# Sliding-window attention and a mixture of adapters on one core: Q kept by rows, a longer warm-up, the last group in halves, and a new written-out order

## The chip, the cores and the metric

The kernel runs on one core of a Trainium2 chip. A core has five engines that run side by side and wait for each other by semaphores: TensorE (PE: matmuls and the weight loads ahead of them), VectorE (DVE), ScalarE (ACT), GpSimd (POOL) and SyncE (SP). Each works through its own instructions strictly in order. Transfers between memory (HBM) and the on-chip SBUF are issued from an engine's queue and run on 16 DMA engines that all queues share. Matmuls write to PSUM, which the kernel uses as 8 banks of 512 float32 words a partition.

The metric is the time of one execution in microseconds (us), as the device reports it.

## What is computed

Inputs are q, k and v of shape (8, 8, 576, 64): batch, heads, sequence, width, in float32. Attention is limited to a window of 32 positions to each side. Its output, with heads side by side as x of 4608 rows and 512 columns, goes through a mixture of 8 adapters of rank 16, of which each row takes the two with the largest logits:

```
scores = q @ k.T / sqrt(64);  scores[|i - j| > 32] = -1e9
x      = (softmax(scores) @ v), heads side by side        # [4608, 512]
logits = x @ w_gate;  top 2 of 8;  w = softmax of these two
out    = x + sum over the two e of  w[e] * ((x @ A[e]) @ B[e])
```

## The kernel before, in words

A unit is one batch entry and head. The 64 units are laid out as two halves of partitions (g = 0, 1: batch entries 0 to 3 and 4 to 7) of 32 units, and these are worked off in two passes p = 0, 1 of NU = 16 units. The 576 rows are cut into NB = 9 blocks of 64.

Loading (`load_qk`, `load_v`). Q and K come in tiles t of 128 rows for 16 units of each half, t = 0 to 3 for pass 0, t = 4 to 7 for pass 1, and t = 8 (`XT`) holds what is left at the ends of all units. One tile is two loads of 256 KB (four of 128 KB for Q's t = 8), issued from POOL's queue (L305), which turn float32 into float16 on the way. V's tiles come as four loads of 128 KB each (L383). For t in `DIRECT` = (0, 1, 8), PE transposes the raw tile itself (L319, 16 transposes of 64 columns for each half hf); for the others POOL, now and then ACT, first brings it into another order (`cast`, L331 and L329), and PE takes 8 transposes of 128 columns for a half (L339). ACT or DVE then copies PSUM into qT or kT in SBUF (`evict`, L356). POOL or ACT copies the end rows of Q from xq into qT (`ends`, L365). DVE transposes V (L391). qT lies as [partition, unit, row], so one unit's rows are adjacent; a pair of rows lies as one float32 word, and evictions move words.

Scores (`score`). For each pass, block a and half of the units, PE adds the window's mask (two matmuls of 512 columns with the constants mask and twice, L425) and then, for 8 units and both g, multiplies K's block with the 64 to 128 Q rows that can see it (L435: 16 matmuls, 32 for the block in the middle, where Q goes from one qT tile to the next). ACT takes the exponential into PT (L444). There are 36 such score groups.

PV (`pv`). For each pass and group g of 128 rows (five groups of a pass), PE multiplies PT with V and a column of ones, in three portions of 6, 5 and 5 units (L480); DVE takes the reciprocal of the sums (L491) and multiplies into x (L497).

Adapters (`moe`), once for each of the 10 groups, over four tiles of 128 rows: PE transposes x (L526), ACT copies (L181), PE multiplies with the adapters' A and w_gate (L566), DVE takes maximum and differences (L576, L577), ACT the exponential (L584), DVE seven small operations (L590 to L597) and the product with the gates (L607), PE transposes (L616), ACT or DVE copies (L181, L179), PE multiplies with B (L640), and x is added. That last step goes two ways for each pair of row tiles: where `BY_PE` (L684) says so, PE adds x through a matmul with the identity (L643) and ACT or DVE only copies to ob (L651); elsewhere DVE adds (L654). SP stores ob (L661), 40 stores in all.

The order of all this is written out. The functions above only record operations in a `Plan`; `ORDER` is the list in which `Plan.give` emits all 566 of them, `ON` picks the engine of each that can go to two, and `HOME` gives each buffer its place in its pool (raw tiles, cast tiles c16, PSUM banks B, x, and so on; pool sizes in `POOLS`). No operation may be emitted before those that make what it needs, or before the last holder of its buffer is done. The waits themselves are set by the recording layer below, from which part of a tile an instruction touches: where the ranges of addresses of two accesses overlap, the later one waits, even if the two leave out each other's elements. Loads from POOL use 8 semaphores in turn, and a load waits until the one before it on its semaphore has landed.

At the start PE runs `WARM` = 4 matmuls of 512 columns in float32 on zeros (L222).

## Time and profile before

| | us |
|---|---|
| median of 3 runs | 130.28 |
| lowest and highest | 129.54, 130.38 |
| the profiled execution | 131.63 |
| its span, first to last instruction | 129.7 |

The profile records that one execution. Its page has the busy time of each engine; the span in 40 slices of 3.24 us, each digit the busy share in tenths; the DMA queues; the chain of work that ended last, followed back from the end, as shares; and groups of instructions by line. PEld are PE's weight loads. A row of the timeline reads: start, duration, engine, line, what is written and read, the count of instructions, and in brackets the idle time before it with what ended it. A row of the windows reads: stretch, its length, the busy time of each engine with its instructions, the clock that TensorE was granted (1 is full speed), the DMA engines' share, and what they moved. A row of the groups ends in busy time, mean ns of one, and idle time before it by what ended it.

### The profile page before, as it was taken

What the parts mean: (1) busy time and instruction counts of PE and PEld (TensorE: products, weight loads), DVE (VectorE), ACT (ScalarE), POOL (GpSimd) and SP (SyncE); (2) the same over time, 40 slices, a digit from 0 to 9 for tenths busy, and PEclk for the clock granted to TensorE, in tenths of its full rate; (3) what the DMA queues carried; (4) which work ended last, traced back from release to release, by engine and by line L of the source; (5) the groups of instructions that cost most, each with busy time, mean ns of one, the idle gap of its engine ahead of it and who ended that gap; (6) DMA issues with size and microseconds to landing.
All of it is one profiled execution on the core that took longest, in us unless ns stands there. A gap on an engine that the chain in (4) does not pass through costs nothing.

```text
span 129.7 us, 5424 instructions
## 1 busy us (share of the span) xinstructions
PE 110.1 (85%) x2354; PEld 80.8 (62%) x2354; DVE 90.9 (70%) x204; ACT 81.2 (63%) x127; POOL 65.0 (50%) x119
## 2 busy tenths in 40 slices
PE   6904987978899999979699999999999999988620
PEld 3204955657778667667595577899767677855200
DVE  4000605749995899959779579979799896898830
ACT  6001354959868758965577978678868976644430
POOL 6879619629896999194983386991000000000000
PEclk9997579999999999999999999999999999999996
DMA  4999996999999999999999999989025036365684
GB/s 91 195 199 211 209 187 95 164 192 203 184 194 214 192 135 234 212 231 281 251 254 206 215 251 203 157 233 323 27 61 181 13 121 224 111 199 189 234 287 181
DMA packets 13542, 24.47 MB, mean 189 GB/s; under 512 B 3024, under 2 KB 3024, under 8 KB 13520
## 3 DMA queue, kind: packets, MB, share of 16 engines
q0 software_dynamic: 6944, 14.16, 61.5%
q1 hardware_dynamic: 5248, 9.44, 20.7%
q10 hardware_dynamic: 1328, 0.54, 1.8%
q8 instruction: 18, 0.29, 0.9%
q14 instruction: 4, 0.03, 0.1%
HBM read 28.85 MB, written 9.44 MB: 295 GB/s over the span
## 4 chain that ended last, share of the span: by engine, by line
PE 49%; DMA 26%; POOL 11%; ACT 4%; issue 4%; DVE 1%; SPq 0%; POOLq 0%
DMA raw<-in_q_dram 24%; PE banks L435 9%; PE banks L480 8%; PE banks L566 6%; PE banks L339 6%; PE banks L526 5%; PE banks L640 5%; POOL raw L305 5%; PE banks L425 4%; POOL c L331 3%; PE banks L319 3%; POOL v L383 3%; ACT ob L651 2%; PE banks L643 2%; DMA out_dram<-ob 2%
## 5 line engine op out<-in xcount | busy, mean ns | idle before, releaser
L444 ACT ACTIVATE PT<-banks 128x1024 f16<-128x1024 f32 x36 | 35.8, 1025 | 9.9 <-PE banks L435 9.0
L331 POOL COPY c<-raw 128x1024 f16<-128x1024 f16 x22 | 22.9, 1066 | 8.9 <-DMA raw<-in_k_dram 3.8
L497 DVE TENSOR_TENSOR x<-banks,rc 128x640 f16<-128x640 f32 (+1 forms) x30 | 25.8, 866 | 0.9
L435 PE MATMUL banks<-qT,kT 64*64 64x128 f16 (+2 forms) x640 | 23.0, 214 | 1.4 <-DVE qT L356 0.8
L435 PEld LDWEIGHTS <-kT 64*64 64x64 f16 x640 | 17.4, 108 | 10.4 <-issue 9.2
L383 POOL DMA_DIRECT2D v<-in_v_dram x36 | 18.4, 522 | 5.7 <-DMA raw<-in_k_dram 3.9
L480 PE MATMUL banks<-vt,PT 64*128 64x65 f16 x832 | 17.4, 190 | 1.7 <-issue 0.9
L391 DVE STREAM_TRANSPOSE vt<-v 128x1024 f32<-128x1024 f32 x9 | 18.7, 2080 | 0.1
L480 PEld LDWEIGHTS <-PT 64*128 64x128 f16 x832 | 14.3, 94 | 4.9 <-issue 3.0
L339 PE MATMUL banks<-ident,c 128*128 128x128 f16 x192 | 13.9, 220 | 2.2 <-issue 1.1
L425 PE MATMUL banks<-mask,twice 64*128 64x512 f16 x72 | 14.4, 389 | 0.4 <-issue 0.3
L640 PE MATMUL banks<-Bw,zT 128*128 128x512 f16 x40 | 13.0, 382 | 1.4 <-ACT zT L181 1.4
L654 DVE TENSOR_TENSOR ob<-banks,x 128x1024 f32<-128x1024 f32 x11 | 13.4, 1217 | 0.6 <-PE banks L640 0.4
L339 PEld LDWEIGHTS <-c 128*128 128x128 f16 x192 | 11.2, 98 | 3.8 <-issue 1.3
L356 DVE COPY qT<-banks 128x512 f32<-128x512 f32 x3 | 2.0, 670 | 16.2 <-PE banks L319 16.2
L319 PE MATMUL banks<-ident,raw 128*64 128x128 f16 x192 | 8.4, 251 | 4.8 <-DMA raw<-in_q_dram 4.8
L305 POOL DMA_DIRECT2D raw<-in_q_dram x20 | 10.8, 560 | 2.6 <-DMA raw<-in_q_dram 1.2
L491 DVE RECIPROCAL rc<-banks 128x10 f32<-128x10 f32 (+1 forms) x30 | 6.4, 215 | 8.1 <-PE banks L480 6.1
L356 ACT COPY kT<-banks 128x512 f32<-128x512 f32 x16 | 9.3, 594 | 4.3 <-PE banks L339 3.4
L526 PE MATMUL banks<-ident,x 128*128 128x128 f16 x160 | 11.5, 220 | 0.2 <-DVE x L497 0.2
L181 ACT COPY xT<-banks 128x512 f32<-128x512 f32 x20 | 11.2, 593 | 0.6 <-PE banks L526 0.4
L356 ACT COPY qT<-banks 128x512 f32<-128x512 f32 x13 | 7.5, 594 | 6.4 <-PE banks L339 3.8
(55 smaller groups left out, 135.3 us busy)
## 6 DMA issues: line engine op xcount, KB each, us to landing
out_dram<-ob SPq DMA_DIRECT2D x24, 256.0 KB, 4.3
raw<-in_k_dram POOLq DMA_DIRECT2D x18, 256.0 KB, 7.2
v<-in_v_dram POOLq DMA_DIRECT2D x36, 128.0 KB, 6.4
raw<-in_q_dram POOLq DMA_DIRECT2D x16, 256.0 KB, 7.8
out_dram<-ob SPq DMA_DIRECT2D x16, 192.0 KB, 3.9
raw<-in_q_dram POOLq DMA_DIRECT2D x4, 128.0 KB, 5.5
ob<-in_moe_A_dram ACTq DMA_DIRECT2D x1, 256.0 KB, 3.0
ob<-in_moe_B_dram ACTq DMA_DIRECT2D x1, 256.0 KB, 5.6
```

The costliest lines, as they stand in the source:

```text
L331: (nc.vector if eng == "DVE" else nc.gpsimd).tensor_copy(out=o, in_=i)
L339: nc.tensor.matmul(out=ap16(tp)[:, 128 * r:128 * r + 128], lhsT=ap(c16)[:, r], rhs=ident, is_transpose=True, start=True, stop=True)
L356: (nc.vector.tensor_copy if eng == "DVE" else nc.scalar.copy)(out=o, in_=i)
L383: op("POOL", 0.5, lambda p0=p0, src=src: nc.gpsimd.dma_start(out=ap(v16)[p0:p0 + 32], in_=src), bufs=[v16], make=[("v", t, "16")], prio=-6 ...
L391: nc.vector.transpose(out=o, in_=i)
L425: nc.tensor.matmul(out=ps_[:, 4 * j:4 * j + 4], lhsT=twice[m], rhs=bcast(mask[m], 1, 4), start=True, stop=False)
L435: nc.tensor.matmul(out=ps_[m, h, o0:o0 + c1 - c0], lhsT=ap(kT[t])[m, 64 * sl:64 * sl + 64], rhs=ap(qT[p, hq])[m, i, c0 - 288 * hq:c1 - 288 ...
L444: op("ACT", act(1024), lambda: nc.scalar.activation(out=ap(pt)[:, :, 64:192].rearrange("m i (x b r) -> m i x b r", b=2, r=16), in_=ap(ps). ...
L480: nc.tensor.matmul(out=ap(po)[:, 512 * g + VD * j:512 * g + VD * j + VD], lhsT=ap(PT[ti])[m, pos, off:off + 128], rhs=ap(vt[t])[m, sl, 0:V ...
L497: nc.vector.tensor_tensor(out=o, in0=i, in1=ap(rc)[:, 0:n].to_broadcast([128, n, 2, D]), op=ALU.mult)
L526: nc.tensor.matmul(out=ap16(tp)[:, 512 * i + 128 * c:512 * i + 128 * c + 128], lhsT=xp()[:, ab, bl].rearrange("p (m c) -> p c m", c=4)[:, ...
L640: nc.tensor.matmul(out=o, lhsT=ap(zT)[:, j + i], rhs=Bw, start=True, stop=not by_pe)
```

## The change

- `qT` is laid out as [partition, x, r, unit] instead of [partition, unit, row]: runs x of 32 rows, in these 16 pairs of rows r, in these the 16 units, and in these the pair of rows b. `evict` and `ends` write so. A score matmul reads its moving operand as pairs of float16 that lie 64 bytes apart, where it read up to 128 adjacent ones; what it writes stays.
- `WARM` goes from 4 to 8. Pool c16 goes from 6 to 7 tiles.
- The last group (pass 1, g = 4) is cut in two halves by units: four PV portions of 4 units instead of three, a second x buffer for the second half, and two calls of `moe` with two row tiles each instead of one with four.
- Which engine adds x follows from `ON`: where ACT takes the last step of a pair, PE adds x; where DVE takes it, DVE adds. In the new `ON`, ACT takes 10 of the 20 pairs and DVE 10; before, ACT took 8 and DVE 12, one of the 12 only copying.
- `ORDER`, `ON` and `HOME` are new throughout, with 576 operations. At the start the loads come as the first part of Q's tile 8, the first of K's tile 0, the rest of Q's tile 8, the second of K's tile 0, Q's tile 0, then V's tile 0, K's tile 1, Q's tile 1 (before: Q's tile 8 and tile 0 and K's tile 0 mixed, Q's tile 1, K's tile 1, V's tile 0). The copy of the first end rows goes from POOL to ACT. All four score groups of blocks 0 and 1 come ahead of the transposes of tile 1. In pass 1, Q's tiles 6 and 7 are loaded ahead of K's tiles 6 and 7, which were loaded ahead of or among them. The last operations are the two halves of group 4, where group 3 was the last.
- Of the operations with a choice, DVE takes 1 copy of Q where it took 4, 4 of K where it took 2, 2 of the transposed x where it took none and 4 of the transposed zs where it took 1. POOL casts 22 tile halves as before.

The diff without the three tables:

```diff
@@ -117,7 +119,7 @@
     assert tuple(q.shape) == (8, NH, NB * 64, D)
     DD = out.shape[1]
-    POOLS = {"B": 8, "raw": 6, "c16": 6, "v16": 3, "xq": 1,
+    POOLS = {"B": 8, "raw": 6, "c16": 7, "v16": 3, "xq": 1,
              "qT": 3, "kT": 3, "vt": 4, "PT": 8, "x": 3, "xT": 2, "zs": 2, "zT": 2, "ob": 4,
              "sm": 2, "rc": 3}
     sb = tc.alloc_tile_pool(name="sb", bufs=1)
@@ -131,7 +133,7 @@
         "c16": many("c16", [128, 8, 2 * D], F16),
         "v16": many("v16", [128, 32 * D], F16),
         "xq": many("xq", [128, 2048], F16),
-        "qT": many("qT", [128, NU, NB * 32], F16),
+        "qT": many("qT", [128, NB * 32 * NU], F16),
         "kT": many("kT", [128, 2048], F16),
         "vt": many("vt", [128, 32, VD2], F16),
         "PT": many("PT", [128, 8, 256], F16),
@@ -306,7 +308,7 @@
                 out=ap(raw)[p0:p0 + np_, g], in_=src),
                bufs=[raw], make=[(w, t, "raw")],
                prio=(-80 + due + late if t else -200 + late) + 0.01 * n,
-               dma=DMA_MB * 0.53 * np_ / 128, desc=np_)
+               dma=DMA_MB * 0.48 * np_ / 128, desc=np_)
         for hf in range(2):
             tp = buf("B", f"tp{w}{t}_{hf}")
             if t in DIRECT:
@@ -340,16 +342,15 @@
                                          rhs=ident, is_transpose=True,
                                          start=True, stop=True)
             pr = due - 22 + late + 0.1 * hf
-            op("PE", 8 * mm(128), trans, bufs=[src, tp], need=[token, "ident"],
+            op("PE", 0.58 if t in DIRECT else 8 * mm(128), trans, bufs=[src, tp], need=[token, "ident"],
                make=[(w, t, hf, "T")], prio=pr, count=n)
             def evict(eng, hf=hf, tp=tp):
                 if w == "q" and t < XT:
-                    c0 = (16, 80, 0, 64)[t % 4]
-                    o = ap(dst).bitcast(F32)[:, :, c0:c0 + 64].rearrange(
-                        "m u (x f r) -> m f u x r", f=2, r=8)[:, hf]
-                    i = ap(tp).rearrange("m (r u x) -> m u x r", r=8, u=NU)
+                    x0 = (1, 5, 0, 4)[t % 4]
+                    o = ap(dst).bitcast(F32).rearrange("m (x f r u) -> m f x r u", f=2, r=8, u=NU)[:, hf, x0:x0 + 4]
+                    i = ap(tp).rearrange("m (r u x) -> m x r u", r=8, u=NU)
                 else:
                     o = ap(dst).bitcast(F32).rearrange("m (x f r) -> m f x r", f=2, r=8)[:, hf]
                     i = ap(tp).rearrange("m (r x) -> m x r", r=8)
@@ -360,7 +361,7 @@
     def ends(p, e):
         def go(eng):
-            o = ap(qT[p, e]).bitcast(F32)[:, :, 128 * e:128 * e + 16]
+            o = ap(qT[p, e]).bitcast(F32).rearrange("m (x r u) -> m x u r", r=16, u=NU)[:, 8 * e]
             i = ap(xq).bitcast(F32).rearrange("m (e u r) -> m e u r", e=2, r=16)[:, e, NU * p:NU * p + NU]
             (nc.scalar.copy if eng == "ACT" else nc.gpsimd.tensor_copy)(out=o, in_=i)
         op({"POOL": 0.45, "ACT": act(256)}, 0, go, bufs=[xq, qT[p, e]], need=[("qT", XT)],
@@ -432,9 +433,10 @@
                     o0 = c0 - (64 * a - 32)
                     for g in range(2):
                         m = slice(64 * g, 64 * g + 64)
-                        nc.tensor.matmul(out=ps_[m, h, o0:o0 + c1 - c0],
+                        qx = ap(qT[p, hq])[m].rearrange("m (x r u b) -> m u x r b", r=16, u=NU, b=2)
+                        nc.tensor.matmul(out=ps_[m, h, o0:o0 + c1 - c0].rearrange("m (x r b) -> m x r b", r=16, b=2),
                                          lhsT=ap(kT[t])[m, 64 * sl:64 * sl + 64],
-                                         rhs=ap(qT[p, hq])[m, i, c0 - 288 * hq:c1 - 288 * hq], start=False,
+                                         rhs=qx[:, i, (c0 - 288 * hq) // 32:(c1 - 288 * hq) // 32], start=False,
                                          stop=h % 4 == 3 and c1 == hi)
         n = len(cuts) - 1
         dur = mm(512) + 0.02 + 8 * (mm(hi - lo) + 0.004 * n)
@@ -455,13 +457,14 @@
     xs = {}
     for p in range(SP):
         for g in range(5):
-            xs[p, g] = buf("x", f"x{p}{g}")
+            xs[p, g] = [buf("x", f"x{p}{g}")] * 2
+    xs[SP - 1, 4] = [xs[SP - 1, 4][0], buf("x", f"x{SP - 1}4b")]
     def pv(p, g, i0, n):
         token = (p, g, i0)
         po, rc = buf("B", f"po{token}", 2), buf("rc", f"rc{token}")
-        xd = xs[p, g]
+        xd = xs[p, g][i0 // 8]
         ops, bufs, need = [], {po}, set()
         mine = [(a, off) for a, off in ((2 * g - 1, 128), (2 * g, 64), (2 * g + 1, 0)) if 0 <= a < NB]
         for j, i in enumerate(range(i0, i0 + n)):
@@ -496,21 +499,21 @@
             o = ap(xd)[:, :, D * i0:D * (i0 + n)].rearrange("p a (n d) -> p n a d", d=D)
             nc.vector.tensor_tensor(out=o, in0=i, in1=ap(rc)[:, 0:n].to_broadcast([128, n, 2, D]), op=ALU.mult)
         op("DVE", dve32(128 * n), norm, bufs=[po, rc, xd], need=[("rc", token)],
-           make=[("x", p, g)], prio=pr)
+           make=[("x", p, g, b) for b in range(2) if i0 < 8 * b + 8 and i0 + n > 8 * b], prio=pr)
     for p in range(SP):
         for g in range(5):
-            for i0, n in ((0, 6), (6, 5), (11, 5)):
+            for i0, n in ((0, 6), (6, 5), (11, 5)) if (p, g) != (SP - 1, 4) else ((0, 4), (4, 4), (8, 4), (12, 4)):
                 pv(p, g, i0, n)
-    def moe(p, g, p0, step):
-
-        items = [(ab, bl) for bl in range(2) for ab in range(2)]
-        tok = (p, g)
+    def moe(p, g, bls, p0, step):
+
+        items = [(ab, bl) for bl in bls for ab in range(2)]
+        tok = (p, g, bls[0])
         xT = buf("xT", f"xT{tok}")
         n = len(items)
-        xd = xs[p, g]
+        xd = xs[p, g][bls[0]]
         def xp():
@@ -529,7 +532,7 @@
                             rhs=ident, is_transpose=True, start=True, stop=True)
             pr = p0 + step * 0.2 * j
             op("PE", 4 * len(two) * mm(128), turn, bufs=[xd, tp],
-               need=[("x", p, g)], make=[("tx", tok, j)], prio=pr, count=4 * len(two))
+               need=[("x", p, g, two[0][1])], make=[("tx", tok, j)], prio=pr, count=4 * len(two))
             def evict(eng, j=j, m=len(two), tp=tp):
                 o = ap(xT)[:, j:j + m].rearrange("p b c m -> p (b c m)")
@@ -539,7 +542,7 @@
                make=[("xT", tok, j)], prio=pr)
         sm = buf("sm", f"sm{tok}")
-        pzs = [buf("B", f"pz{tok}", 2)]
+        pzs = [buf("B", f"pz{tok}", n // 2)]
         zss = [buf("zs", f"zs{tok}")]
         nw = len(pzs)
@@ -576,7 +579,7 @@
                 nc.vector.tensor_reduce(out=m1[:, w], in_=lg, axis=AX.X, op=ALU.max)
                 nc.vector.tensor_tensor(out=d[:, w], in0=lg, in1=bcast(m1[:, w], 2, E),
                                         op=ALU.subtract)
-            op("DVE", 0.4, gate0, bufs=[pz, sm], need=[("pz", tok, w)], make=[("g0", tok)],
+            op("DVE", 0.36 + 0.01 * n, gate0, bufs=[pz, sm], need=[("pz", tok, w)], make=[("g0", tok)],
                prio=pr + w)
         def gexp():
@@ -595,7 +598,7 @@
             nc.vector.tensor_tensor(out=g, in0=e, in1=bcast(m2, 3, E), op=ALU.is_ge)
             nc.vector.tensor_tensor(out=e, in0=e, in1=bcast(sv, 3, E), op=ALU.mult)
             nc.vector.tensor_tensor(out=g, in0=e, in1=g, op=ALU.mult)
-        op("DVE", 1.5, gate2, bufs=[sm, pzs[0]], need=[("g2", tok)], make=[("g3", tok)], prio=pr + 1)
+        op("DVE", 1.2 + 0.02 * n, gate2, bufs=[sm, pzs[0]], need=[("g2", tok)], make=[("g3", tok)], prio=pr + 1)
         for w, pz in enumerate(pzs):
             mine = list(range(n))
@@ -632,9 +635,11 @@
                 def x_of(pair=pair, m=m):
                     return xp()[:, :, pair[0][1]]
-                by_pe = BY_PE(p, g, j)
-
-                def delta(j=j, m=m, pd=pd, zT=zT, x_of=x_of, by_pe=by_pe):
+
+                taker = []
+
+                def delta(j=j, m=m, pd=pd, zT=zT, x_of=x_of, taker=taker):
+                    by_pe = taker[0].on == "ACT"
                     for i in range(m):
                         o = ap(pd)[:, 512 * i:512 * i + 512]
                         nc.tensor.matmul(out=o, lhsT=ap(zT)[:, j + i], rhs=Bw,
@@ -642,18 +647,18 @@
                         if by_pe:
                             nc.tensor.matmul(out=o, lhsT=ident, rhs=x_of()[:, i],
                                              start=False, stop=True)
-                op("PE", m * mm(512) * (2 if by_pe else 1), delta, bufs=[pd, zT, xd],
-                   need=[("zT", tok, w), "Bw"], make=[("pd", dt)], prio=pq, count=m * (2 if by_pe else 1))
-
-                def add(eng, pd=pd, ob=ob, m=m, x_of=x_of, by_pe=by_pe):
+                first = op("PE", m * mm(512), delta, bufs=[pd, zT, xd],
+                           need=[("zT", tok, w), "Bw"], make=[("pd", dt)], prio=pq, count=m)
+
+                def add(eng, pd=pd, ob=ob, m=m, x_of=x_of):
                     i0 = ap(pd).rearrange("p (i c) -> p i c", c=512)
-                    if by_pe:
-                        (nc.vector.tensor_copy if eng == "DVE" else nc.scalar.copy)(
-                            out=ap(ob)[:, 0:m], in_=i0)
+                    if eng == "ACT":
+                        nc.scalar.copy(out=ap(ob)[:, 0:m], in_=i0)
                     else:
                         nc.vector.tensor_tensor(out=ap(ob)[:, 0:m], in0=i0, in1=x_of(), op=ALU.add)
-                op({"ACT": act(512 * m), "DVE": dve32(512 * m)} if by_pe else {"DVE": dve32(512 * m)}, 0, add,
-                   bufs=[pd, ob, xd], need=[("pd", dt)], make=[("ob", dt)], prio=pq)
+                taker.append(op({"ACT": act(512 * m), "DVE": dve32(512 * m)}, 0, add,
+                                bufs=[pd, ob, xd], need=[("pd", dt)], make=[("ob", dt)], prio=pq))
+                first.link, first.more = taker[0], (m * mm(512), m)
                 for i, (ab, bl) in enumerate(pair):
                     def store(i=i, ob=ob, ab=ab, bl=bl):
                         lo, hi = (32 if g == 0 else 0), (96 if g == 4 else 128)
@@ -663,7 +668,8 @@
     for p in range(SP):
         for g in range(5):
-            moe(p, g, 144 * p + (32 * g + 46 if g < 4 else 158), 4)
+            for bls in ((0, 1),) if (p, g) != (SP - 1, 4) else ((0,), (1,)):
+                moe(p, g, bls, 144 * p + (32 * g + 46 if g < 4 else 158) + bls[0], 4)
     tc.plan = P
     if ORDER:
@@ -675,71 +681,68 @@
 LATE_W = -150
-WARM = 4
+WARM = 8
 LOAD = 0.56
 DIRECT = (0, 1, 8)
 CAST = {"POOL": 1.04, "ACT": 1.03}
-def BY_PE(p, g, j):
-
-    return (p > 0 or g > 1) and j > 0 or (p, g) == (1, 4)
-
 ORDER = (
...
```

18 lines of the change are left out of this document (10 added, 8 removed), and 85 rows, old and new, of tables (HOME, ORDER).

## The prediction

> **What bounds the kernel now.** I read the page first: busy times, the 40 slices and the shares of the chain.
>
> ```profile
> span 129.7 us, 5424 instructions
> ...
> PE 110.1 (85%) x2354; PEld 80.8 (62%) x2354; DVE 90.9 (70%) x204; ACT 81.2 (63%) x127; POOL 65.0 (50%) x119
> ...
> PE   6904987978899999979699999999999999988620
> ...
> PE 49%; DMA 26%; POOL 11%; ACT 4%; issue 4%; DVE 1%; SPq 0%; POOLq 0%
> ```
>
> TensorE (PE) is busy nearly without a break from slice 16 (52 us) to slice 36, and half of the chain is PE work. Before that the chain is DMA and POOL, and PE has holes. So there are three places to win: the holes before 52 us, PE work itself, and the tail after slice 36. The windows give the holes a size.
>
> ```profile
> core 0: us, PE busy (x) PEld busy (x) DVE busy (x) ACT busy (x) POOL busy (x), PEclk, DMA share, GB/s
> 10.00:15.00 5.00, 3.62 (x77) 3.35 (x79) 1.39 (x4) 1.17 (x2) 4.73 (x16) 0.61 1.12 210
> 15.00:20.00 5.00, 4.56 (x80) 3.13 (x77) 0.74 (x3) 2.50 (x4) 1.08 (x3) 0.71 0.92 176
> 20.00:25.00 5.00, 3.89 (x103) 3.04 (x100) 3.48 (x8) 3.38 (x6) 4.96 (x11) 1.00 0.84 129
> 25.00:35.00 10.00, 8.16 (x261) 6.70 (x257) 7.97 (x14) 8.34 (x13) 6.09 (x11) 1.00 1.08 193
> 55.00:65.00 10.00, 8.04 (x206) 6.40 (x206) 7.41 (x18) 5.80 (x10) 7.85 (x11) 1.00 1.09 257
> 13.60:124.40 110.80, 102.33 (x2296) 76.47 (x2292) 89.29 (x197) 77.99 (x123) 54.09 (x87) 0.98 0.85 188
> ```
>
> From 20 to 35 us PE lacks 1.11 + 1.84 = 2.95 us, from 55 to 65 another 1.96. Between 10 and 20 us it runs at a granted clock of 0.61 and 0.71. POOL works only 1.08 of the 5 us after 15, and just behind it the DMA falls to 129 GB/s. The timeline of the first 40 us says why.
>
> ```profile
> 1.09 5.28 PE L222 MATMUL banks<-zw 128*128 128x512 f32 x8 [1.09 <-DVE zw L217]
> 5.35 0.19 PEld L222 LDWEIGHTS banks<-zw 128*128 128x128 f32 x1 [0.24 <-issue]
> 6.73 0.52 POOL L305 DMA_DIRECT2D raw<-in_q_dram  x1 [0.57 <-DMA raw<-in_q_dram]
> 10.17 1.05 PE L319 MATMUL banks<-ident,raw 128*64 128x128 f16 x31 [2.55 <-DMA raw<-in_q_dram]
> 12.42 3.84 PE L319 MATMUL banks<-ident,raw 128*64 128x128 f16 x64 [1.20 <-DMA raw<-in_q_dram]
> 14.38 0.59 ACT L356 COPY qT<-banks 128x512 f32<-128x512 f32 x1 [2.54 <-PE banks L319]
> 16.94 1.06 PE L435 MATMUL banks<-qT,kT 64*64 64x128 f16 x16
> 18.04 1.02 ACT L444 ACTIVATE PT<-banks 128x1024 f16<-128x1024 f32 x1 [0.85 <-PE banks L435]
> 19.07 0.40 POOL L365 COPY qT<-xq 128x256 f32<-128x256 f32 x1 [3.84 <-ACT PT L444]
> 22.36 0.48 PE L435 MATMUL banks<-qT,kT 64*64 64x96 f16 x14 [0.82 <-DVE qT L356]
> 29.29 0.63 PE L435 MATMUL banks<-qT,kT 64*64 64x128 f16 x16
> 38.12 0.63 PE L435 MATMUL banks<-qT,kT 64*64 64x128 f16 x16
> ```
>
> Two waits come from the layout of Q. POOL's copy of the end rows (L365) idles 3.84 us: it writes rows of qT which the scores of block 1 do not read, but with units outermost every access spans the whole tile, so it stands behind both score groups issued ahead of it. The load issues of v, k and q queued behind it on POOL stand too, and the DMA runs dry. Likewise the scores of block 0 wait 0.82 us for the eviction of Q tile 1, which they do not read.
>
> **The change, part by part.** The durations that I use come from the chain of waits at full clock, from the groups by line (the first number is their busy time, the second the mean ns of one) and from the page's DMA issues (KB of one, us to landing).
>
> ```profile
> 83.70 0.89 PE banks L339 x16
> 89.22 0.89 PE banks L526 x16
> 91.95 0.32 PE banks L425 x2
> 92.27 0.56 PE banks L435 x16
> ...
> 119.57 0.22 PE banks L643
> ```
>
> ```profile
> L526 PEld LDWEIGHTS <-x 128*128 128x128 f16 x160 | 9.8, 114 | 1.5 <-issue 0.4 <-DVE x L497 0.3
> L339 PEld LDWEIGHTS <-c 128*128 128x128 f16 x192 | 11.2, 98 | 3.8 <-issue 1.3 <-POOL c L331 0.9 <-ACT c L329 0.3
> L654 DVE TENSOR_TENSOR ob<-banks,x 128x1024 f32<-128x1024 f32 x11 | 13.4, 1217 | 0.6 <-PE banks L640 0.4
> L594 DVE RECIPROCAL sm<-banks 128x4 f32<-128x4 f32 x10 | 1.8, 182 | 0.3
> L356 DVE COPY qT<-banks 128x512 f32<-128x512 f32 x3 | 2.0, 670 | 16.2 <-PE banks L319 16.2
> L356 DVE COPY kT<-banks 128x512 f32<-128x512 f32 x2 | 1.3, 660 | 0.8 <-PE banks L319 0.8
> L179 DVE COPY zT<-banks 128x512 f16<-128x512 f16 x1 | 0.4, 415 | 0.0
> ```
>
> ```profile
> raw<-in_k_dram POOLq DMA_DIRECT2D x18, 256.0 KB, 7.2
> v<-in_v_dram POOLq DMA_DIRECT2D x36, 128.0 KB, 6.4
> ```
>
> *Warm-up of 8.* The last of its passes, two a matmul, are 0.19 + 0.24 = 0.43 us apart (row at 5.35). Four more matmuls add 8 x 0.43 = 3.4 us to 1.09 + 5.28 = 6.37: 9.8 us. The first Q load is whole only at 10.17, so nothing waits for it; only if the passes went on at the cold pace would the warm-up end after that, and each us beyond would be one of start-up. PE's idle stretch of 3.8 us, after which the clock is 0.61, goes. 32 transposes take half of 3.84 = 1.92 us cold and 1.05 / 31 x 32 = 1.08 warm; the 16 matmuls of a score group 1.06 cold (at 16.94) and 0.56 warm (at 92.27). If a short gap should still cost the clock, all of it, 2 x 0.84 + 0.5 = 2.2 us, is lost again.
>
> *Q by runs of rows, then units.* Evictions and end copies move as many elements, 0.59 and 0.40 us: nothing, bounded by the 0.07 us between the DVE's copies of q and k (670 and 660 ns, one stride order against the other). The false waits go. The cost can lie in the scores: the moving operand was 128 adjacent f16 and becomes 64 pairs, 64 bytes apart. No row of before has a strided moving operand. The nearest is the strided stationary one of L526 (one f16 in four), beside the adjacent one of L339: both take 0.89 us for 16. That is one end, 0. A weight load is hidden behind its matmul while a moving read is not; the other end is the difference of the loads alone, 114 against 98 ns, 16% on 0.56 x 36 groups = 3.2 us. I take 0, as both rows read two values in 16 bytes, and keep 3.2 for the range. [...]
>
> *The order up to the scores of block 5.* Loads: the same eight parts come first, but the second half of Q tile 0 is now the last. A 256 KB part at 210 GB/s (10 to 15 us) takes 1.25 us, a 128 KB part 0.62. PE started on it at 12.42; now 13.65. Its transposes end 1.08 later at 14.75, the last eviction (ACT, 0.59 and two hand-overs) at 15.45. POOL must have built the second constant by then. It is queued behind the issue for Q tile 1, which waits for a landing (as at 6.73) until 12.4; with 0.55 for the issue and 2.5 of building it ends at 15.45, a tie. A score group is 0.32 + 0.56 = 0.88, so the first ends at 16.4 (before: 16.94 + 1.06 = 18.0), and four in a row at 18.9. Before, the fourth ended at 22.84 with 1.08 of other work among them: 2.9 ahead. Now v0, k1 and q1 land until 13.65 + 4 x 0.62 + 4 x 1.25 = 21.15. PE has k1's transposes and two PV groups to fill that; then it stands in order before q1's transposes, with everything behind it. They end at 22.25, their evictions 0.7 later (22.95), and the next four score groups with two transposes of x run from 23.3 to 27.3; before, the last of them ended at 29.92 without those transposes (0.9): 3.5 ahead. ACT, with an exponential of 1.02 behind each group, is full here. POOL has no end copy to wait for, since the first of these is now on ACT; its issues stay ahead of the DMA. With the same work done, the first score group of block 5 ends at 34.7 by this count, before at 38.75: **4.0 us**.
>
> *The rest of the order.* Loads come 3 to 4 us earlier, but so does PE; I take half of the 1.96 us of holes at 55 to 65: **1.0 us**. Behind 65 us PE is full either way, so a better order finds no hole there. The same 74 loads and 40 stores are issued, on POOL and SP as before, and share the DMA: k4, k6 and k7 move behind v and q parts on POOL, and the seventh cast buffer lets one cast more go ahead of PE. SP only orders the stores, none of which anything waits for but an ob buffer; that costs nothing while four of these are there, and an add (1.0 on ACT) if they are not.
>
> *The engine that adds x.* ACT takes 10 pairs instead of 8 (before, DVE copied one that PE had added, so PE had 9). One pair more is two matmuls of 0.22 on PE: **+0.4 us**.
>
> *DVE.* It gives up two adds and three q evictions, and takes two k, two xT and three zT evictions, a PV group, and nine small gate instructions more: -2 x 1.22 - 3 x 0.67 + 2 x 0.66 + 2 x 0.66 + 3 x 0.42 + 0.4 + 9 x 0.18 = +1.5 us, and 0.5 for small ones: 2.0. From 13.6 to 124.4 DVE works 89.3 of 110.8 us; some 200 hand-overs of 0.04 (row to row in its tail) leave it 13 us free. In a stretch 4.5 us shorter with 2.0 more work it has 7. Between nothing and the whole gain I take **+1.2 us** given back by an engine that is in order and nearly full.
>
> *The last group in two halves.*
>
> ```profile
> 111.04 1.91 PE L480 MATMUL banks<-vt,PT 64*128 64x65 f16 x96
> 115.05 0.81 DVE L497 TENSOR_TENSOR x<-banks,rc 128x640 f16<-128x640 f32 x1
> 123.99 1.01 ACT L651 COPY ob<-banks 128x1024 f32<-128x1024 f32 x1 [1.56 <-DMA out_dram<-ob]
> ```
>
> Before, from the last PV matmul (112.95) to the end are 16.75 us: 2.9 until x is whole (115.86), then 13.84 of chain, stores included. A chain for half is transposes 0.6, eviction 0.65, logits 0.6, gates 2.4, transpose and eviction 0.75, delta 0.6, add 1.25 and, as before, 129.7 - 125.0 = 4.7: 11.6; and with two norms of 0.7 and a reciprocal ahead of it, 13.3. But PE's own work behind the last PV falls, at 0.056 us a transpose, 0.22 a delta matmul and 0.06 a logit matmul, from 7.9 (32 logits, 28 transposes, 20 deltas) to 5.4 (16, 24, 14), so that PV ends 2.5 later: 16.75 - 13.3 - 2.5, about **0.9 us** gained. The PV groups of this group are four of 16 matmuls for 24 + 20 + 20: the same 64. Two x buffers let the first half's transposes start while the other half is still normed.
>
> Sum: -4.0 - 1.0 + 0.4 + 1.2 - 0.9 = -4.3. The profiled execution took 131.63 us, 1.9 around its span of 129.7, and is 1.0% above the median of 130.28; its span becomes 125.4, its time 127.3, and the median 130.28 - 4.3 = **126.0**.
>
> **The rivals.**
>
> *The strided moving operand runs at half speed* (the slower side). Eight concurrent pairs of 128 columns take 0.56 us now; read at half speed a group takes 0.86. 36 x 0.30 = 10.7 us on the engine that bounds: 136.7. It decides from 4.3 / 36 = 0.12 us a group, 0.68 instead of 0.56. For it speaks that a moving read hides behind nothing; against it the equal 0.89 of L339 and L526.
>
> *DVE becomes the bound.* If the order leaves it idle nearly as large a share of the time as now (10% where it was 13), the stretch lasts (89.3 + 2.0 + 8.2) / 0.9 = 110.5 instead of 110.8, and the end is about 130.0. Its norm at 115.05, two us behind the PV that it belongs to, speaks for it.
>
> *Loads of the second half come late.* k6 and k7 now stand almost last on POOL, behind casts of q6 and q7 that wait for PE to free cast buffers. By my count they are cast about 2 us before PE needs them; 5 us of misjudged stores would stop PE for 3 and undo the holes won: 126.0 + 5 = 131.
>
> *The clock falls in spite of the warm-up*: 126.0 + 2.2 = 128.2.
>
> **How the numbers follow.** Main case 60%, 126.0, its own range 122.8 (the full 1.96, no DVE loss, a better tail) to 129.2 (+3.2 for the reads). DVE 12%, loads 10%, clock 5%, half speed 13%. The range runs to 132, which takes in all but the half speed and a little at the lower end. About 1%, 1.3 us, is what a measurement can tell from no change. Faster than 129.0: 60 + 5 and a quarter of DVE, 68%; within 1%: the rest of DVE and part of the loads, 13%; slower: 19%.
>
> **What would show it.** Right: granted clock of 1.00 from 10 to 20 us, no POOL idle of several us before 25, the first exponential at about 16.4, score groups of 16 at 0.56 in the chain, PE lacking under 1 us in 55 to 65, a last chain under 12 us. Wrong: score groups of 0.68 or more; PE waits on DVE in the second half; PE idle before the transposes of k6 or k7.

## The result, and the profile after

The changed kernel takes 139.48 us, the median of 5 runs (138.95 to 140.26), beside 130.28 us (129.54 to 131.36) of the kernel before: a ratio of 1.069, 95% interval 1.063 to 1.076. It is slower by about 9 us; 126.0 us, faster by 4.3, was forecast, with a range up to 132. The rest of this text is from the profiled runs and from twelve further kernels. Executions of one and the same kernel differ by up to 4%, so the times below, where a kernel ran several times, are medians of its fast runs, those within 1.5% of its fastest, and each ratio to before compares fast runs alone.

The page of the kernel after (busy times, then the shares of the chain that ended last):

```profile
span 137.4 us, 5452 instructions
...
PE 126.0 (92%) x2364; PEld 91.1 (66%) x2364; DVE 93.4 (68%) x220; ACT 82.9 (60%) x125; POOL 65.3 (48%) x119
...
PE 79%; DMA 5%; POOL 4%; DVE 4%; issue 3%; ACT 1%; POOLq 0%; DVEq 0%; ACTq 0%
PE banks L437 24%; PE banks L483 11%; PE banks L426 8%; PE banks L341 8%; PE banks L569 7%; PE banks L529 7%; PE banks L645 7%; DMA raw<-in_q_dram 5%; PE banks L648 3%; PE banks L321 2%; POOL raw L307 2%; PE banks L619 2%; POOL twice L209 1
```

The span is 7.7 us longer, PE's busy time 15.9 us, some 4 of it the longer warm-up (9.42 us against 5.28). PE now holds 79% of the chain where it held 49%, and a single line, the score matmuls (L437, before L435), is a quarter of it. The long waits of before on DMA and POOL (26% and 11%) are nearly gone from the chain. That could be taken for a success of the new order, but it says nothing about the time: with matmuls at full rate the chain of the same order reads much the same (PE 73%, DMA 6%, POOL 4%, in a_units_inside below), at 131.04 us. The same line by the shapes of its matmuls, in the kernel after:

```profile
L437 PE MATMUL banks<-qT,kT 64*64 64x128 f16 x384 | 25.2, 282 | 0.0
L437 PE MATMUL banks<-qT,kT 64*64 64x96 f16 x128 | 6.7, 257 | 0.0
L437 PE MATMUL banks<-qT,kT 64*64 64x64 f16 x128 | 4.3, 229 | 0.0
```

and two steps of its chain of waits at full clock, a mask pair and a score group of 16:

```profile
99.94 0.32 PE banks L426 x2
100.27 0.98 PE banks L437 x16
```

The mask pair takes 0.32 us as before. The score group takes 0.98, before 0.56 (the row at 92.27 in the prediction). So the same 16 matmuls over the same 128 columns, at the same clock, need 0.42 us more; all that has changed in them is where Q's elements lie. The mean of 282 ns hides this in part: it is the time from start to modelled end of one matmul, with others in flight beside it (16 of them add up to 4.5 us and take 0.98). The chain's group shows the rate.

The start, in the timeline of the kernel after (start, us, engine; in brackets what was waited for and how long):

```profile
1.09 9.42 PE L224 MATMUL banks<-zw 128*128 128x512 f32 x16 [1.09 <-DVE zw L219]
10.44 2.44 PE L321 MATMUL banks<-ident,raw 128*64 128x128 f16 x65
13.68 2.25 POOL L209 TENSOR_SCALAR_AFFINE_SELECT twice<-twice 64x32 f16<-64x32 f16 x8
13.89 1.08 PE L321 MATMUL banks<-ident,raw 128*64 128x128 f16 x31 [1.01 <-DMA raw<-in_q_dram]
15.99 0.60 PE L426 MATMUL banks<-mask,twice 64*128 64x512 f16 x1 [0.70 <-POOL twice L209]
16.53 0.86 PE L437 MATMUL banks<-qT,kT 64*64 64x96 f16 x16
17.42 1.02 ACT L446 ACTIVATE PT<-banks 128x1024 f16<-128x1024 f32 x1 [1.78 <-PE banks L437]
```

and in its windows (columns as in the prediction: window, busy time of PE, PEld, DVE, ACT and POOL, then granted clock, DMA share, GB/s):

```profile
10.00:15.00 5.00, 3.86 (x99) 3.01 (x97) 2.37 (x5) 1.65 (x3) 3.50 (x10) 1.00 1.10 210
15.00:20.00 5.00, 4.30 (x54) 2.40 (x53) 2.42 (x3) 2.69 (x4) 4.46 (x11) 0.66 1.11 207
```

PE waits 1.01 us for the last part of Q and 0.70 us for POOL's second constant, and the clock drops just behind, though the warm-up ran to 10.51: in steps of 1 us it is 1.00 up to 15, 0.99 to 16 and 0.50 from 16 to 19, which makes the 0.66.

### The profile page after: what moved, and what is told of

Read it like the earlier page. It is cut to its first block, busy times and chain, and to the rows that moved or that the text cites. A ratio compares the mean times of both kernels' runs of the same rounds, so it can differ in the third digit from the quotient of the medians.

```text
span 137.4 us, 5452 instructions
## 1 busy us (share of the span) xinstructions
PE 126.0 (92%) x2364; PEld 91.1 (66%) x2364; DVE 93.4 (68%) x220; ACT 82.9 (60%) x125; POOL 65.3 (48%) x119
## 3 DMA queue, kind: packets, MB, share of 16 engines
q0 software_dynamic: 6944, 14.16, 57.3%
q1 hardware_dynamic: 5248, 9.44, 19.8%
HBM read 28.85 MB, written 9.44 MB: 279 GB/s over the span
## 4 chain that ended last, share of the span: by engine, by line
PE 79%; DMA 5%; POOL 4%; DVE 4%; issue 3%; ACT 1%; POOLq 0%; DVEq 0%; ACTq 0%
PE banks L437 24%; PE banks L483 11%; PE banks L426 8%; PE banks L341 8%; PE banks L569 7%; PE banks L529 7%; PE banks L645 7%; DMA raw<-in_q_dram 5%; PE banks L648 3%; PE banks L321 2%; POOL raw L307 2%; PE banks L619 2%; POOL twice L209 1%; DVE ob L658 1%; DVE x L500 1%
## 5 line engine op out<-in xcount | busy, mean ns | idle before, releaser
L437 PE MATMUL banks<-qT,kT 64*64 64x128 f16 (+2 forms) x640 | 36.1, 267 | 0.0
L437 PEld LDWEIGHTS <-kT 64*64 64x64 f16 x640 | 27.4, 120 | 8.9 <-issue 8.7
L500 DVE TENSOR_TENSOR x<-banks,rc 128x640 f16<-128x640 f32 (+2 forms) x31 | 26.1, 843 | 1.1
L494 DVE RECIPROCAL rc<-banks 128x10 f32<-128x10 f32 (+2 forms) x31 | 6.6, 213 | 12.1 <-PE banks L483 10.8
L645 PE MATMUL banks<-Bw,zT 128*128 128x512 f16 x40 | 13.3, 382 | 1.3 <-ACT zT L183 0.8
L658 DVE TENSOR_TENSOR ob<-banks,x 128x1024 f32<-128x1024 f32 x10 | 12.0, 1221 | 3.2 <-PE banks L645 3.1
L183 ACT COPY xT<-banks 128x512 f32<-128x512 f32 x18 | 10.2, 591 | 5.1 <-PE banks L529 5.0
L569 PE MATMUL banks<-WA,xT 128*128 128x136 f16 x160 | 11.5, 223 | 1.1 <-issue 0.6
L656 ACT COPY ob<-banks 128x1024 f32<-128x1024 f32 x10 | 10.1, 1016 | 2.3 <-PE banks L648 2.2
L569 PEld LDWEIGHTS <-xT 128*128 128x128 f16 x160 | 9.7, 98 | 2.7 <-ACT xT L183 1.2
L307 POOL DMA_DIRECT2D raw<-in_k_dram x18 | 9.8, 551 | 2.4 <-PE banks L321 1.5
```

Of the source, the lines that this page charges most:

```text
L307: op("POOL", LOAD, lambda g=g, p0=p0, np_=np_, src=src: nc.gpsimd.dma_start(out=ap(raw)[p0:p0 + np_, g], in_=src), bufs=[raw], make=[(w, t ...
L437: nc.tensor.matmul(out=ps_[m, h, o0:o0 + c1 - c0].rearrange("m (x r b) -> m x r b", r=16, b=2), lhsT=ap(kT[t])[m, 64 * sl:64 * sl + 64], r ...
L500: nc.vector.tensor_tensor(out=o, in0=i, in1=ap(rc)[:, 0:n].to_broadcast([128, n, 2, D]), op=ALU.mult)
L569: nc.tensor.matmul(out=ap(pz)[:, o:o + ER + E], lhsT=ap(xT)[:, i, c, :], rhs=WA[:, c, :], start=(c == 0), stop=(c == 3))
L645: nc.tensor.matmul(out=o, lhsT=ap(zT)[:, j + i], rhs=Bw, start=True, stop=not by_pe)
```

## The experiments

Theories. **S**: the moving operand as pairs of f16, 64 bytes apart, is read slowly, and this alone makes the kernel slower. **D**: it is not the distance but the access pattern of several dimensions. **O**: the matmuls are not the cause; the new order, its waits and its evictions cost the time. The first four kernels make a table of layout and order.

**The new order, Q in whole runs** (a_units_inside): the dimensions of the pattern stay, but a row run of 32 f16 is adjacent.

```diff
-  qx = ap(qT[p, hq])[m].rearrange("m (x r u b) -> m u x r b", r=16, u=NU, b=2)
+  qx = ap(qT[p, hq])[m].rearrange("m (x u r b) -> m u x r b", r=16, u=NU, b=2)
```

(the evictions and end copies alike)

> The changed kernel whole, with its order, warm-up and halves; only inside a run of 32 rows the units come before the rows, so a score matmul reads 32 adjacent f16 (64 bytes), then jumps 1024 bytes. The pattern has as many dimensions as in the changed kernel, and runs of rows are still outermost. Theory S (reading pairs 64 bytes apart slows the moving operand): 16 matmuls take 0.56 us again instead of 1.04, and the time falls by about 36 x 0.46 = 16.6 from 139.5 to 123 (121 to 126). Theory D (the pattern of several dimensions slows, whatever the distance): 139. Theory O (the new order, its waits or the evictions slow, not the reads): 139.

Measured: 131.04 us, ratio to before 1.011 (0.994 to 1.027). Its page, and its score matmuls by shape:

```profile
span 129.0 us, 5452 instructions
...
PE 113.6 (88%) x2364; PEld 81.5 (63%) x2364; DVE 93.0 (72%) x220; ACT 81.5 (63%) x125; POOL 65.0 (50%) x119
...
PE 73%; issue 7%; DVE 6%; DMA 6%; POOL 4%; ACT 1%; DVEq 0%; POOLq 0%; ACTq 0%
```

```profile
L437 PE MATMUL banks<-qT,kT 64*64 64x128 f16 x384 | 16.0, 223 | 1.5 <-issue 1.5
```

The matmuls are back at 223 ns: with equal dimensions but adjacent runs the slowness is gone. D falls, and O falls as the cause of the slower time. But the time came back only to that of before, not to the 123 us that S expected by giving the new order its forecast gain. So there are two findings to explain: a loss in the layout, and a missing gain. (The 123 also took 0.46 us a group in full for the loss; by the chain it is 0.42, and not all of it reaches the time.)

**The new order, the old layout** (a_old_layout: tile, evictions, end copies and read of before).

> The changed kernel with the layout of Q of before (units outermost), all else changed. Theory S: score groups at 0.56 again, about 123 plus what the waits for overlapping ranges cost in an order that was not made for them, 0 to 4: 123 to 127. Theory D: the same, since the pattern has one dimension again. Theory O: 139 or more.

Measured: 130.20 us, ratio 1.004 (0.992 to 1.017), span 129.0, 223 ns; again not the 123 to 127 of S and D. The false waits of the old layout, which the new layout lifts, cost nothing that can be measured in this order.

**The old order, the new layout** (b_pairs).

> The kernel before with only the new layout of Q (runs, pairs of rows, units): its old order, warm-up, last group. Theories S and D: 130.3 + 16.6 less 0 to 2 for waits that go = 145 to 147. Theory O: 128 to 130.

Measured: 138.95 us, ratio 1.071 (1.028 to 1.114); slower, as S and D said, but by 6 to 8 us less than they said.

```profile
L435 PE MATMUL banks<-qT,kT 64*64 64x128 f16 x384 | 25.1, 282 | 0.5 <-ACT kT L355 0.4
```

**The old order, Q in whole runs** (b_units_inside: as b_pairs, with 32 adjacent f16).

> The kernel before with Q in runs of 32 rows, in these the units, in these the rows; nothing else. Theory S: score groups stay at 0.56; the two waits on overlapping ranges go (3.84 us of POOL, 0.82 of PE), worth 0 to 3 us: 127.5 to 130.5. Theory D: 145. Theory O: 127.5 to 130.5.

Measured: 128.73 us, ratio 0.991 (0.975 to 1.007), 223 ns. So pairs cost 8.4 us in the new order (139.48 against 131.04) and 10.2 in the old (138.95 against 128.73). All else of the change shows no gain: with the old layout the ratio is 1.004, and with whole runs the new order (1.011) stands behind the old (0.991), though with intervals that overlap.

**What makes a moving read slow.** Five kernels with the order of before and the layout of b_pairs read the score's moving operand from other places of the same Q rows, so that they leave out the attention of this input: runs of 1 to 8 adjacent f16 at a fixed step. One of them:

```diff
-  qx = ap(qT[p, hq])[m].rearrange("m (x r u b) -> m u x r b", r=16, u=NU, b=2)
+  qx = ap(qT[p, hq])[m].rearrange("m (x g s) -> m x g s", x=NB, s=4)
...
-  rhs=qx[:, i, (c0 - 288 * hq) // 32:(c1 - 288 * hq) // 32], start=False,
+  rhs=qx[:, xa:xb, 0:16, 0:2], start=False,
```

> The order of before, with Q laid out in pairs as the change does; the score matmuls read other elements of the same row runs of Q (so the output is not attention of this input): pairs of f16, one pair in every 8 bytes. Before, 32 adjacent f16: 223 ns mean of the 64x128 form and 0.56 us for 16 of them in the chain; pairs 64 bytes apart: 282 ns and 0.98 us. Theory R (a run of only 4 bytes is what costs, at any distance): 282 ns and 0.98 us, about 139 us in all. Theory L (what counts is how many values lie in each 16 bytes read; here 4 of 8): between, 0.56 to 0.8 us. Theory B (a distance of 64 bytes is what costs): 223 ns and 0.56 us, about 130 us.

> As the run with a pair in every 8 bytes, but one pair in every 16 bytes. R: 0.98 us for 16 matmuls, 282 ns. L: as pairs 64 bytes apart, which also have one pair in each 16 bytes that they touch: 0.98 us. B: 0.56 us, 223 ns, about 130 us.

> As the runs before it, but runs of 4 f16 (8 bytes), one in every 64 bytes. R: between 0.56 and 0.98 us, since the run is twice as long. L: the same as one pair in every 8 bytes, since 4 values of 8 are read of each 16 bytes. B: 0.98 us, 282 ns, about 139 us.

> As the runs before it, but runs of 8 f16 (16 bytes), one in every 64 bytes. L: 0.56 us and 223 ns, since each 16 bytes touched are used whole. R: 0.56 us or a little over it. B: 0.98 us, 282 ns, about 139 us.

> As the run with one pair in every 16 bytes (two f16 of each 16 bytes, 290 ns for the 64x128 form and 1.02 us for 16), but the two f16 apart: one f16 in every 8 bytes, again other elements of Q than the reference's. If the number of values read of each 16 bytes counts: again 280 to 300 ns and about 1.0 us. If it is the number of 4-byte words touched in each 16 bytes (here two, as with a pair in every 8 bytes): 223 ns and 0.56 us. If the length of the run counts: slower than 1.02 us.

Each ran once, so the group of matmuls is the measurement, not the whole time. By shape, in this order: a pair in 8 bytes, a pair in 16, four f16 in 64, eight in 64, a single one in 8:

```profile
L436 PE MATMUL banks<-qT,kT 64*64 64x128 f16 x384 | 15.9, 221 | 0.5 <-ACT kT L355 0.4
```

```profile
L436 PE MATMUL banks<-qT,kT 64*64 64x128 f16 x384 | 26.2, 290 | 0.5 <-ACT kT L355 0.4
```

```profile
L436 PE MATMUL banks<-qT,kT 64*64 64x128 f16 x384 | 15.4, 217 | 0.8 <-ACT kT L355 0.8
```

```profile
L436 PE MATMUL banks<-qT,kT 64*64 64x128 f16 x384 | 15.2, 219 | 0.5 <-ACT kT L355 0.4
```

```profile
L436 PE MATMUL banks<-qT,kT 64*64 64x128 f16 x384 | 26.2, 289 | 0.3 <-ACT kT L355 0.2
```

| f16 read of each 16 bytes touched | arranged as | ns of one | us for 16 in the chain | whole time, us |
|---|---|---|---|---|
| 2 | pairs 64 bytes apart (b_pairs) | 282 | 0.98 | 139.0 |
| 2 | pairs 16 bytes apart | 290 | 1.02 | 140.5 |
| 2 | single ones 8 bytes apart | 289 | 1.02 | 141.3 |
| 4 | pairs 8 bytes apart | 221 | 0.57 | 133.7 |
| 4 | runs of 4, 64 bytes apart | 217 | 0.56 | 129.6 |
| 8 | runs of 8, 64 bytes apart | 219 | 0.56 | 128.4 |

The distance does not count (64 bytes is fast with four values, 16 slow with two), nor the run's length (a pair is slow or fast by its neighbours), nor the number of words of 4 bytes touched (two words are slow as two single values, fast as two pairs). What sorts these rows is how many values are read of each 16 bytes: with four 16 matmuls take 0.56 to 0.57 us, with two 0.98 to 1.02. Neither 8 nor 32 bytes would sort the rows: of each 8 bytes touched, a slow row and a fast one both read a pair (pairs 64 and 8 bytes apart), and of each 32 both read four values (pairs 16 bytes apart, runs of 4). Three values were not tried, nor another type than f16. The pair in 8 bytes, with matmuls at full rate, still took 133.7 us: its clock fell to 0.78 between 45 and 55 us. A whole time of one run says little about its matmuls.

**Where the gain of the order went.** Theory **T**: the transfers set when data arrive, so an order that starts earlier waits for them later. Theory **P**: the loads are hidden, and the order, the evictions and PE's own work set the time. Two kernels with Q in whole runs load a third less: all loads after the first of each buffer bring half of their bytes (14.16 MB become 9.44; the rest of a tile keeps what an earlier load left there).

```diff
+    def part(x, wt):
+        if wt in (("q", XT), ("q", 0), ("k", 0), ("q", 1), ("k", 1), ("k", 2), ("v", 0), ("v", 1), ("v", 2)):
+            return x
+        n = x.shape[-1] // 2
+        return x[tuple([slice(None)] * (len(x.shape) - 1) + [slice(0, n)])]
...
-                out=ap(raw)[p0:p0 + np_, g], in_=src),
+                out=part(ap(raw)[p0:p0 + np_, g], (w, t)), in_=part(src, (w, t))),
```

(and v alike)

> The order of before with Q in whole rows of 32 f16 (130.6 us), but all loads of Q, K and V after the first of each buffer bring only half of their bytes (the other half of the tile keeps what an earlier load left, so the output is not attention of this input): about a third less is loaded. Theory T (the transfers, which fill the DMA engines from 5 to 85 us, set when data arrive, and so no order of the same loads ends earlier): 123 to 127 us, since PE idles some 10 us between 5 and 65 us and the larger part of it would go. Theory P (the loads are hidden anyway; the order, the evictions and PE's own work set the time): 129 to 131 us.

> The same lighter loads with the new order, warm-up, halves and pair rule, and Q in whole rows of 32 f16 (131.0 us with full loads). T: 120 to 125 us, 2 to 4 us below the old order with the same lighter loads, since what the new order gains at the start is no longer taken back by late loads. P: within 1.5 us of the old order with lighter loads.

Measured: the old order 127.28 us (126.22 to 127.53; ratio to before 0.972, 0.963 to 0.981), the new one 126.05 us (125.37 to 126.39; 0.962, 0.952 to 0.972); spans 125.3 and 124.3. The windows from 35 to 65 us, the old order with full loads and with light ones:

```profile
35.00:45.00 10.00, 9.86 (x265) 7.74 (x263) 7.82 (x22) 7.82 (x14) 9.73 (x16) 1.00 1.06 195
45.00:55.00 10.00, 7.61 (x140) 5.03 (x134) 7.50 (x9) 6.52 (x11) 6.10 (x10) 1.00 1.09 213
55.00:65.00 10.00, 8.90 (x233) 7.29 (x232) 7.68 (x20) 6.27 (x11) 7.81 (x13) 1.00 1.03 212
```

```profile
35.00:45.00 10.00, 10.00 (x269) 7.81 (x266) 8.03 (x23) 8.01 (x15) 10.00 (x17) 1.00 0.68 97
45.00:55.00 10.00, 9.38 (x194) 6.52 (x194) 8.66 (x10) 8.08 (x12) 8.22 (x13) 1.00 0.84 145
55.00:65.00 10.00, 10.00 (x239) 8.44 (x240) 9.29 (x24) 6.63 (x12) 6.59 (x12) 1.00 0.99 212
```

The new order with full loads (here to 75 us, for what follows) and with light ones:

```profile
35.00:45.00 10.00, 9.29 (x219) 6.76 (x216) 8.34 (x26) 7.27 (x11) 8.62 (x14) 1.00 1.09 199
45.00:55.00 10.00, 9.36 (x199) 6.57 (x198) 9.17 (x8) 5.86 (x10) 7.85 (x13) 1.00 1.05 189
55.00:65.00 10.00, 7.81 (x250) 6.87 (x244) 6.61 (x21) 7.32 (x13) 6.71 (x10) 1.00 1.10 262
65.00:75.00 10.00, 9.15 (x156) 7.42 (x154) 8.07 (x19) 6.33 (x12) 9.17 (x15) 1.00 1.06 261
```

```profile
35.00:45.00 10.00, 10.00 (x240) 7.38 (x236) 8.76 (x22) 7.46 (x12) 9.78 (x16) 1.00 0.78 119
45.00:55.00 10.00, 10.00 (x261) 7.33 (x260) 9.44 (x13) 7.20 (x11) 10.00 (x17) 1.00 1.04 195
55.00:65.00 10.00, 8.40 (x201) 7.59 (x198) 8.29 (x20) 7.32 (x13) 9.96 (x15) 1.00 0.67 133
```

With full loads the DMA engines are busy throughout (a share of 1.03 to 1.10) and PE lacks 3.63 us under the old order, 3.54 under the new. With a third less to load the share is 0.67 to 1.04 and PE lacks 0.62 and 1.60, one profile each. So fewer bytes take away the larger part of these holes, whatever the order, and P, which left the old order at 129 to 131 us, falls there. In time the old order gains 1.4 us by it (128.73 with full loads), the new one 5.0 (131.04). T does not come out whole either: both times lie a little above what it gave, and the new order leads by 1.2 us with ranges that overlap a little, not by 2 to 4; 1.2 is within the 1.5 that P gave. Most of what the new order was thought to win is not there to be taken back.

Nor do the traces show PE waiting for data in most of these holes, as T had it. Two of them in the chain of the new order with whole runs and full loads (start, us, what), and a DMA queue on its page (packets, MB, share):

```profile
55.17 0.51 PE banks L483 x26
55.68 0.93 issue
56.61 0.34 PE banks L483 x10
...
67.68 0.47 PE banks L569 x8
68.15 0.85 issue
69.00 0.63 PE banks L569 x8
```

```profile
q8 instruction: 18, 0.29, 0.8%
```

Both holes stand inside groups of like matmuls, and "issue" is time in which the profile shows nothing that was waited for. From 35 to 75 us, 3.60 of the 4.39 us that PE lacks in this kernel are put down to "issue". The queue named instruction brings 18 packets of 16 KB through the same DMA engines. By the packets' start times in the traces of all fourteen kernels, each of the 39 idle stretches of PE behind 20 us that are put down to "issue" and last 0.2 us or more ends 2.2 to 2.8 us after one of these packets starts. So does the hole of 2.39 us behind 48 us under the old order with full loads, which the profile puts down to DVE (2.26 us). A PE that waits for its own instructions, whose transfer comes late among the loads, would fit. That is the author's guess from coinciding times and is not shown: no kernel here changes the instructions alone.

**A warm-up of 4** in the new order with whole runs (d_after_warm4; `WARM = 4`).

> The new order with Q in whole rows of 32 f16, with a warm-up of 4 in place of 8. If the longer warm-up is worth what the prediction took it for (a clock of 1.00 from 10 us on): 1 to 3 us longer than the 131.0 us with 8. If it only fills time in which PE waits for the first Q and K anyway: within 1 us, and the clock about 0.65 to 0.75 in 10 to 20 us as before.

Measured: 130.25 us, ratio to before 0.997 (0.992 to 1.002), beside the 1.011 (0.994 to 1.027) with 8. The clock is 0.66 in 10 to 15 us and 1.00 in 15 to 20, the other way round than with 8. The longer warm-up shows no gain.

## Why the prediction was wrong, step by step

**Q by runs of rows, then units: costed at 0, with 3.2 us as its upper bound. This step failed.** By the chain it costs 0.42 us for 24 of the groups, 0.30 for the 8 at the ends (0.76 against 0.46) and 0.38 for the 4 in the middle (1.00 against 0.62): 14 us of PE work over 36 groups, and 8.4 to 10.2 us of time. In the new order the difference is mostly PE idle time that filled up: against the same order with whole runs PE is busy 12.4 us longer (126.0 - 113.6), and idle 11.4 us instead of 15.4, which leaves 8.4, the difference of the spans. The row that the 0 rested on, L526 beside L339, was about the stationary operand, whose loads run beside the matmuls (16 take 0.89 us with loads of 114 ns and with loads of 98 ns); it could not bound a moving read. Nor do "both rows" read two values in 16 bytes: L526 does, but L339 reads adjacent ones. The prediction said so itself ("a weight load is hidden behind its matmul while a moving read is not") and then bounded the moving read by weight loads all the same: 16% was the most it allowed, 75% was measured. A cost that no row of before shows should have been given a wide end and more than 13%. That two values in 16 bytes cost nothing was the author's assumption, and no run shows the 0 that went into the sum: at two f16 of each 16 bytes a group of 16 takes 0.98 to 1.02 us (the kernel after, b_pairs, c_4_of_16, c_2_of_8), at four 0.56 to 0.57 (c_4_of_8, c_8_of_64).

**The rival "strided moving operand at half speed"** is what happened. It gave 0.86 us a group, the author's estimate, and 136.7 us; the group was 0.98. Its 136.7 was near the 139.5 by luck, as its errors partly cancelled: it took 0.30 for 0.42 us a group, charged every group in full (10.7 us; 8.4 measured), and counted from 126.0, where the rest of the change in fact ends at about 131.

**Start and order to block 5: -4.0 us.** This was mis-sized: some 2.2 us came, and the layout alone brings as much to the old order. The first score group of block 5, in the timelines of the old order with whole runs, the new order with a warm-up of 8, with one of 4, and the kernel after:

```profile
35.80 0.63 PE L435 MATMUL banks<-qT,kT 64*64 64x128 f16 x16
```

```profile
35.97 0.63 PE L437 MATMUL banks<-qT,kT 64*64 64x128 f16 x16
```

```profile
34.72 0.63 PE L437 MATMUL banks<-qT,kT 64*64 64x128 f16 x16
```

```profile
37.49 1.05 PE L437 MATMUL banks<-qT,kT 64*64 64x128 f16 x16
```

It ends at 36.43, 36.60, 35.35 and 38.54; in the profiled run of before at 38.75, and 34.7 was forecast. The new order with the old layout (a_old_layout) ends it at 36.38 (35.74 + 0.64). So the order brings this point 2.2 to 2.4 us forward on before's profiled run, the new layout with its lifted waits does the same for the old order (36.43), and both together do no more. Part of it may be a slow start of that one run, whose clock was 0.50 for 6.8 us from 11.1 on; but under the old order with whole runs and light loads the clock was 0.50 for as long, from 9.2 on, and the group ended at 36.56. In the pieces: the transposes of the last Q part came as counted (13.89 to 14.97, forecast 13.65 to 14.75). The tie with POOL's constant (15.45) was lost: it was ready at 15.93, PE stood 0.70 us, the clock fell to 0.66, and the first exponential started at 17.42 instead of 16.4, before at 18.04. The long warm-up ended at 10.51 and not at 9.8, without harm: with a warm-up of 4 the transposes behind it start at 10.49, when their data come. A clock of 1.00 from 10 to 20 us was forecast; it was 1.00 to 15 only. The rival "the clock falls anyway" came true in this run, with 0.66 in 15 to 20 us; what it cost was not measured by itself.

**The rest of the order: -1.0.** None of it came. PE lacks 2.19 us at 55 to 65 in the new order with whole runs, 1.96 before. Over 35 to 75 us it lacks 0.71 + 0.64 + 2.19 + 0.85 = 4.39, against 2.44 before (rows of before, which with the one at 55 in the prediction give 0.09 + 0.10 + 1.96 + 0.29):

```profile
35.00:45.00 10.00, 9.91 (x211) 7.84 (x209) 7.98 (x24) 7.29 (x13) 8.66 (x13) 1.00 1.08 200
45.00:55.00 10.00, 9.90 (x238) 6.98 (x230) 9.59 (x11) 8.25 (x15) 7.46 (x13) 1.00 1.03 191
65.00:75.00 10.00, 9.71 (x205) 6.66 (x202) 7.67 (x19) 7.76 (x12) 4.67 (x10) 1.00 1.10 220
```

So 1.95 of the 2.2 us of lead are given back here; the old order with whole runs, as early at block 5, lacks 3.86 in these windows. The prediction took the holes for data that come late, and did not ask what the DMA share of 1.0 to 1.1 from 25 to 85 us meant. With full loads the holes come back whoever is early, and nearly all of them end 2.2 to 2.4 us after a packet of instructions starts; with a third less to load they are 0.62 and 1.60 from 35 to 65. The rival "loads of the second half come late" looked for a stop at k6 and k7, which did not come. The prediction also read PE as full from 52 us on, though its slices 18 and 20 are 7 and 6, the holes that it counts at 55 to 65.

**The engine that adds x: +0.4.** Right: 20 matmuls (18 before), 0.22 us apart in the chain.

```profile
L648 PE MATMUL banks<-x,ident 128*128 128x512 f16 x20 | 7.6, 379 | 0.0
```

**DVE: 2.0 us more work.** Right (90.9 to 93.0). Whether it gave back 1.2 us of time was not measured by itself; DVE holds 6% of the chain in the new order with whole runs, 4% in the kernel after and 1% before.

**The last group in halves: -0.9.** Right in size, as far as the profiles tell. The last PV matmuls and the last add, in the new order with whole runs:

```profile
115.23 0.66 PE banks L483 x32
...
123.72 1.22 DVE ob L658
```

From the last PV (115.89) to the end at 129.0 are 13.1 us; 13.3 were forecast, 16.75 stood there before. PV ends 2.94 us later than before, of which 2.5 were forecast. The 0.7 us between 3.65 and 2.94 are the whole difference of the two spans (129.7 and 129.0), the earlier steps included. With those at -2.2 + 1.95 + 0.4 = 0.15, the halves are left with about -0.9, by subtraction from one profile of each. Over more runs, all steps without the layout give no gain that can be told from none (ratio 1.011, 0.994 to 1.027).

What stays open: whether three values in 16 bytes are enough, whether matmuls that don't run as concurrent 64x64 tiles feel the two values as much, what PE's holes inside its groups would be with fewer instructions and the same loads, and how much of before's late start was chance.

## What to carry to other kernels

Before a layout is changed to spare waits, look at the operand that streams: for a moving f16 operand keep at least four values in each 16 bytes read (0.56 to 0.57 us for 16 matmuls here, 0.98 to 1.02 at two), and never take a stationary operand's row as its price (0.89 us for 16 here with one f16 in four and with adjacent ones). Before an order is tuned, look at what PE's holes are put down to, over the whole stretch. Here, with a DMA share of 1.03 to 1.10 and holes inside groups of like matmuls, neither order of the same loads removed them (PE lacked 3.63 and 3.54 us from 35 to 65 us); a third fewer bytes did for the most part (0.62 and 1.60).

## What the runs showed of the hardware

With a moving operand read at two f16 in 16 bytes, 16 matmuls of 64x128 took 0.98 to 1.02 us instead of 0.56: with single values 8 bytes apart 1.02 (c_2_of_8), with pairs 16 bytes apart 1.02 (c_4_of_16), with pairs 64 bytes apart 0.98 (b_pairs). At four in 16 bytes they took 0.57 (c_4_of_8) and 0.56 (c_8_of_64), as with 32 adjacent ones (0.56, a_units_inside).

A warm-up of 9.4 us without a break did not keep the clock for certain. In the kernel after it was 1.00 in 10 to 15 us and 0.66 in 15 to 20, behind two idle stretches of PE of 1.01 us up to 13.89 and 0.70 us up to 15.99. In d_after_light, with a warm-up of 9.07 us and idle stretches of 1.01 and 0.70 us at the same two places, it was 1.00 in both windows; in b_units_inside, with a warm-up of 5.92 us and idle stretches of 2.01 and 1.32 us, as well. Neither the warm-up nor these stretches decide it by themselves.

PE stood idle up to 1.93 us at a time (b_pairs, from 64.76 us), often inside a group of like matmuls, with nothing to wait for that the profile shows. All 39 such stretches of 0.2 us or more behind 20 us, in fourteen traces, end 2.2 to 2.8 us after a 16 KB packet of the queue named instruction starts.
